# First loads in halves, the second batch's k turned on TensorE, and another step order, in an attention kernel with a gated feed-forward

## The chip, the cores and the metric

The kernel runs on one core of one Trainium2 chip. The time is device time in microseconds for one execution of the whole program. The median of three runs of the kernel before the change is 373.25 us (373.04 to 373.4).

## The reference

Eight batches of eight heads with 576 tokens of 64 numbers go through a linear attention with a learned feature map; the result feeds a gated feed-forward layer over all 4608 tokens.

```
def phi(x):
    proj = np.einsum('bhsd,df->bhsf', x, w_phi)               # 64 -> 128
    proj = proj - np.max(np.abs(proj), axis=-1, keepdims=True)
    return np.concatenate([np.exp(proj), np.exp(-proj)], axis=-1)
q_p, k_p = phi(q), phi(k)
kv  = np.einsum('bhsf,bhsd->bhfd', k_p, v)
z   = np.sum(k_p, axis=2)
num = np.einsum('bhsf,bhfd->bhsd', q_p, kv)
den = np.einsum('bhsf,bhf->bhs', q_p, z)[..., None] + 1e-06
x   = (num / den) laid out as [4608, 512]
out = (np.maximum(x @ w_gate, 0.0) * (x @ w_val)) @ w_out     # 512 -> 1536 -> 512
```

## The kernel before

The order of all work is written out by hand: `ORDER` is a string of some two thousand words, and a loop at the end of the kernel calls one small function for each, in that order. A word such as `ke.0.1.3.1:6@kp1` names the function (`do_ke`), its arguments (batch 0, head group 1, chunk 3, sign 1), after the colon the PSUM banks it uses, and after @ the buffer that it takes from a ring. Each engine runs its own instructions strictly in this order; waits between engines follow from the data and the buffers. The transfers stand in the same order on the queue of the engine that issues them: SyncE's queue takes `lf`, `wq`, `lw`, the `lv` of all batches but 0, the transposing transfers `xt` and the outputs `od`; GpSimd's takes `lk`, `lq`, `lm`, `ln`, `wl`, `wo` and batch 0's `lv`, and GpSimd issues them between its own computing.

A batch has 512 "main" tokens, in four chunks of 128, and 64 "rest" tokens. The heads are handled in three groups, `HEADS = ((0, 2), (2, 5), (5, 8))`; group 0 also carries the rest tokens. These are the steps for one batch `b`, group `j`, chunk `i`:

- Loads: `lk`, `lq`, `lv` bring k, q, v; `lm`, `ln`, `lw` bring their rest tokens (`lm` of batch 0 goes to a buffer of its own, `km0`, in another layout than `km`); `lf` brings k of batch 0, group 1 in full precision into a region that later holds `xTm`; `wq` brings `w_phi` twice, into rows 0 to 63 and 64 to 127 of `w64f`; `wl` and `wo` bring the feed-forward weights. Batch 1's v lies in a region that later holds `xTs`.
- Turning k: `kt` (L549) and `ku` (L554) transpose in blocks of 32x32 on VectorE, and `kr` (L565) projects with 24 matmuls of 32 rows and the weights `w32`. Batch 0 goes another way: `k0` (L587) is six 128x128 transposes on TensorE, `k1` (L590) copies them to SBUF on VectorE, and `k3` (L641) projects with six matmuls of 64 rows and the weights `w64`; `do_k2` (twelve such matmuls in one step) is defined and unused. The very first k (`lf`) is turned in full precision by `kf` (L618) and copied by `kg` on VectorE or `kh` on ScalarE. `wd` (L404) makes `w64` out of `w64f`; `sl`, `w1` and `wa` make `w32`.
- `ke` (L661, ScalarE) takes the exponentials of k's projection, `kx` (L669, VectorE) their maxima, `kk` the scale factors, `vs`, `vo`, `vq` (GpSimd) scale v (for batch 0 also `vd`, `vp`, `vz` on VectorE), `kv` (L767) multiplies, and `kc` copies the result to SBUF.
- q: `q0`, `q1`, `qb` (L813) for batch 0, `qt` and `qc` (L827) for the others, then `qe` (ScalarE), `qx` (VectorE) and the small `qy`, `qz`, `qu`, `qw`.
- The quotient: `nu` (L890, TensorE), `nt` (L911) and `nv` (L921) on VectorE, `nr` (L929, the reciprocal), `nx` (L933, GpSimd).
- x is transposed for the feed-forward: `xp` (L970, TensorE) and `xa` (L984, ScalarE) for batch 0, `xt` for the others.
- Feed-forward: `pv` and `pg` (L1093) for batch 0 by quarters of its tokens, `fv` and `fg` (L1064) for the rest, `va`, `ga`, `pa`, `pb` to empty the banks, `fo` (L1125) and the copies `oc`, `oe` to the output.
- `zz.n` (L428) is n matmuls on a tile of zeros that nobody reads: filler in places where TensorE would stand still. They add up to 76.

The first feed-forward matmul in the order is `pv.1.0`. From there on the order mixes the attention of batch b + 1 with the feed-forward of batch b.

## Time and profile before

| | |
|---|---|
| median of three runs | 373.25 us (373.04 to 373.4) |
| the profiled execution | 371.81 us |
| its span, first to last instruction | 370.0 us |
| granted TensorE clock, mean | 1.000 |
| VectorE, ScalarE, GpSimd busy | 289.0, 227.1, 156.5 us |

"PE" is TensorE, "PEld" its weight loads, "DVE" VectorE, "ACT" ScalarE, "POOL" GpSimd, "SP" SyncE; a "q" behind an engine's name means its instruction queue, such as the issue of a transfer. Matmuls overlap in the profile: the duration of one is longer than the distance from its start to the next one's start. VectorE's and ScalarE's instructions overlap by some 0.08 us in the same way. In a timeline a row merges neighbours of one kind (xN), and the brackets give the idle time before it and what ended that.

### The profile page before, as it was taken

The page shows a single profiled execution, that of the slowest core. Times are in us where ns is not written, and L with a number is a line of the kernel's source. Part 1 is how long each engine was busy: PE and PEld are TensorE (multiplying, and loading weights), DVE is VectorE, ACT ScalarE, POOL GpSimd, SP SyncE. Part 2 cuts the span into 40 slices and gives each one's busy share as a digit, 9 for nine tenths or more (in the row PEclk, how much of TensorE's full clock was granted, in tenths as well). Part 3 has the DMA queues.
Part 4 walks back from the last instruction along what each step waited for, and adds up shares of the span by engine and source line. Part 5 has one row for each costly group of instructions (what it writes and reads, how often), then busy time and mean ns, then how long its engine had stood idle before and what let it go on. Part 6 is the DMA issues. An engine that isn't in the chain of part 4 may idle for free.

```text
span 370.0 us, 9211 instructions
## 1 busy us (share of the span) xinstructions
PE 363.5 (98%) x3615; PEld 195.2 (53%) x3615; DVE 289.0 (78%) x674; ACT 227.1 (61%) x550; POOL 156.5 (42%) x161
## 2 busy tenths in 40 slices
...
GB/s 143 258 202 192 179 183 152 172 39 172 110 109 123 159 128 76 86 172 100 58 101 117 14 144 57 37 122 58 127 68 14 2 73 96 48 0 25 33 28 142
DMA packets 90380, 38.09 MB, mean 103 GB/s; under 512 B 64226, under 2 KB 85602, under 8 KB 90338
## 3 DMA queue, kind: packets, MB, share of 16 engines
...
q14 instruction: 14, 0.11, 0.1%
HBM read 37.81 MB, written 9.44 MB: 128 GB/s over the span
## 4 chain that ended last, share of the span: by engine, by line
PE 94%; DVE 2%; DMA 1%; ACT 1%; issue 0%; SPq 0%; ACTq 0%
PE bank L1064 47%; PE bank L1125 25%; PE bank L767 5%; PE bank L890 4%; PE bank L1093 4%; PE bank L565 3%; PE bank L827 2%; DMA w64f<-in_w_phi_dram 1%; PE bank L428 1%; ACT kp L661 1%; DVE h L850 1%; PE bank L1046 1%; PE bank L1156 1%; DVE vr L651 0%; PE bank L813 0%; PE bank L860 0%
## 5 line engine op out<-in xcount | busy, mean ns | idle before, releaser
L1125 PE MATMUL bank<-wo,h 128*128 128x512 bf16 x420 | 97.8, 379 | 0.0
L661 ACT ACTIVATE kp<-bank 128x384 bf16<-128x384 f32 x192 | 84.3, 518 | 15.3 <-PE bank L565 9.9
L1079 ACT CAST val<-bank 128x512 bf16<-128x512 f32 x81 | 47.2, 595 | 73.7 <-PE bank L1064 65.1
L1085 DVE SCALAR_TENSOR_TENSOR h<-bank,val 128x512 bf16<-128x512 f32 x100 | 66.8, 678 | 28.1 <-PE bank L1064 14.2
L1064 PE MATMUL bank<-xTs,wv 128*128 128x512 bf16 x352 | 87.1, 379 | 0.0
L1064 PE MATMUL bank<-xTs,wg 128*128 128x512 bf16 x352 | 86.3, 379 | 0.0
L933 POOL TENSOR_TENSOR xu<-u,r 128x512 bf16<-128x512 f32 x36 | 37.3, 1041 | 96.0 <-DVE r L929 54.3
L842 ACT ACTIVATE qp<-bank 128x512 bf16<-128x512 f32 x128 | 69.2, 620 | 10.7 <-PE bank L827 9.4
L718 POOL TENSOR_TENSOR vs<-vn,ek 128x780 bf16<-128x780 f32 (+2 forms) x40 | 53.7, 1363 | 23.8 <-ACT ek L678 13.3
L1125 PEld LDWEIGHTS <-h 128*128 128x128 bf16 x420 | 39.1, 98 | 45.9 <-issue 2.4
L1064 PEld LDWEIGHTS <-wg 128*128 128x128 bf16 x400 | 37.4, 98 | 41.4 <-issue 0.7
L1064 PEld LDWEIGHTS <-wv 128*128 128x128 bf16 x400 | 36.9, 98 | 40.4 <-issue 0.7
L669 DVE TENSOR_REDUCE mk<-bank 128x3 f32<-128x384 f32 x96 | 49.6, 539 | 2.5 <-ACT kp L661 1.3
L850 DVE TRANSPOSE_TENSOR_REDUCE maxq<-bank 128x16 f32<-128x512 f32 x56 | 37.4, 691 | 6.2 <-ACT qp L842 3.3
L921 DVE TENSOR_TENSOR u<-bank,t 128x195 f32<-128x195 f32 (+1 forms) x108 | 33.8, 329 | 2.8 <-POOL xu L933 0.6
L911 DVE TENSOR_TENSOR t<-bank,cq 128x195 f32<-128x195 f32 (+1 forms) x96 | 30.1, 323 | 6.8 <-PE bank L890 5.9
L890 PEld LDWEIGHTS <-qp 128*128 128x128 bf16 x512 | 23.1, 98 | 12.6 <-issue 2.0
L890 PE MATMUL bank<-kv,qp 128*128 128x65 bf16 x512 | 26.1, 193 | 0.3 <-ACT kv L778 0.2
L1134 ACT COPY ob<-bank 128x512 f32<-128x512 f32 x19 | 11.3, 596 | 22.2 <-PE bank L1125 22.1
L1137 DVE COPY ob<-bank 128x512 f32<-128x512 f32 x16 | 10.9, 683 | 16.1 <-PE bank L1125 13.8
...
L767 PEld LDWEIGHTS <-kp 128*128 128x128 bf16 x640 | 21.6, 97 | 2.8 <-ACT qp L842 0.2
...
## 6 DMA issues: line engine op xcount, KB each, us to landing
out_dram<-ob SPq DMA_DIRECT2D x31, 256.0 KB, 2.4
vn<-in_v_dram SPq DMA_DIRECT2D x24, 256.0 KB, 4.4
kn<-in_k_dram POOLq DMA_DIRECT2D x7, 512.0 KB, 9.2
qn<-in_q_dram POOLq DMA_DIRECT2D x7, 512.0 KB, 7.3
wv<-in_moe_w_val_dram POOLq DMA_DIRECT2D x3, 512.0 KB, 8.8
wg<-in_moe_w_gate_dram POOLq DMA_DIRECT2D x3, 512.0 KB, 8.7
wo<-in_moe_w_out_dram POOLq DMA_DIRECT2D x3, 512.0 KB, 7.6
...
```

Of the source, the lines that this page charges most:

```text
L661: nc.scalar.activation(kp_of(3 * b + j)[:, i, s].rearrange("p n f -> p (n f)"), bank[bk[0]][:, 0 : 3 * F], AF.Exp, scale=(1.0, -1.0)[s],)
L669: nc.vector.tensor_reduce(mk_of(3 * b + j)[:, :, i], bank[bk[0]][:, 0 : 3 * F].rearrange("p (n f) -> p n f", f=F), axis=AX.X, op=ALU.max, ...
L718: nc.gpsimd.tensor_tensor(vs_of(3 * b + j)[:, s, 0:n].rearrange("p n i e -> p (n i) e")[:, :, 0:e], src[:, lo:hi].rearrange("p h i e -> p ...
L767: nc.tensor.matmul(out_ps[:, h - lo, s, :], lhsT=lhsT, rhs=rhs, start=(at == 0), stop=(at == 2 * n * (C + 1) - 1),)
L842: nc.scalar.activation(qp_of(4 * b + i)[:, s, 4 * hq : 4 * hq + 4].rearrange("p h m -> p (h m)"), bank[bk[0]], AF.Exp, scale=(1.0, -1.0)[s],)
L850: nc.vector.tensor_reduce((maxq0[:, i] if b == 0 else maxq)[:, :, i, 4 * hq : 4 * hq + 4].rearrange("p t h -> p h t"), bank[bk[0]].rearran ...
L890: nc.tensor.matmul(bank[bk[0]][:, E * n : E * (n + 1)], lhsT=qp_of(4 * b + i)[:, s, h, :], rhs=kv_of(b)[:, h, s, 0:E],)
L933: eng.tensor_tensor(xu_of(n).rearrange("p (h d) -> p h d", d=D), u_of(n)[:, :, 0:D], r_of(n).to_broadcast([P, H, D]), op=ALU.mult,)
L1064: nc.tensor.matmul(bank[bk[0]], lhsT=w[:, dc, P * f : P * f + P], rhs=xT(g)[:, dc, :], start=(dc == 0), stop=(dc == NDC - 1),)
L1079: nc.scalar.copy(val_of(NFC * g + f), bank[bk[0]])
L1085: nc.vector.scalar_tensor_tensor(h2_of(g, f), bank[bk[0]], 0.0, val_of(NFC * g + f), op0=ALU.max, op1=ALU.mult)
L1125: nc.tensor.matmul(bank[bk[0]], lhsT=h2_of(g, f)[:, P * t : P * t + P], rhs=wo_sb[:, f, :], start=(f == 0), stop=(f == NFC - 1),)
```

## The change

Four things are different. `w_phi` comes in two transfers of 64 rows each, and the first k in two halves of two chunks each; both kinds alternate on SyncE's queue (`lf.1 wq.0 lf.0 wq.1`). Batch 1's k is turned as batch 0's is: three steps `k0.1.j`, `k1.1.j`, `k2.1.j` (twelve matmuls) stand in place of `kt.1.j`, `ku.1` and `kr.1.j`, and its rest tokens go to `km0`. Batch 1's v is loaded by head group with four tokens of a head to a partition (1 KB pieces) in three transfers, where it was loaded by chunks of 128 tokens (256 B pieces) in four. And `ORDER` is another one: up to about batch 2 the steps stand in another sequence, from batch 3 on it is nearly the same sequence with other banks and buffers. The filler adds up to 74 matmuls. The steps that make `w32` (`w1`, `wa`) move from the opening to just before `k2.1.1`.

```diff
--- before.py
+++ after.py
...
-ms.0 lf ms.2 lm.0.0 ms.4@vr0 ms.6 id lk.0.2 lk.0.0 wq ms.3@vr1 if ms.5 zz.12:7 kf.0:0 ms.9 kf.1:1 wd
-kh.0:0@kT0 sl k3.1.0:23 ke.0.1.0.0:2@kp0 w1:4 kg.1:1 kx.0.1.1:3@mk0 kx.0.1.0:2 wa:4 zz.2:7 k3.1.1:56
-ke.0.1.3.0:6 lm.0.1 kx.0.1.2:5 zz.3:7 k0.2:0 lq.0.1 ke.0.1.3.1:6 k1.2:0@kT1 ke.0.1.0.1:2 zz.3:7
-k0.0:1 ke.0.1.2.1:5 ke.0.1.1.1:3 k3.2.1:42 ke.0.1.2.0:5 kx.0.1.3:6 k1.0:1@kT2 zz.5:7 k3.0.1:06
-kk.0.1.0@ek0 k3.0.0:15 ke.0.1.1.0:3 ke.0.0.3.0:6@kp1 q0.1:3 lw.0.1 lq.0.0 kx.0.2.3:2@mk1 kx.0.2.2:4
-kk.0.1.1 ke.0.2.2.0:4@kp2 kx.0.0.0:1@mk2 kx.0.0.2:0 lv.0.1 ke.0.2.2.1:4 ke.0.0.1.1:5 kx.0.0.3:6
-q1.1:3@qT0 ke.0.0.1.0:5 ke.0.0.3.1:6 lv.0.0 zz.6:7 q0.0:4 kx.0.0.1:5 wl.0.1 zz.4:7 k3.2.0:36 lv.0.2
-ke.0.2.3.0:2 ke.0.0.2.1:0 ke.0.0.0.1:1 q1.0:4@qT1 ke.0.2.3.1:2 kx.0.2.1:6 zz.1:7 qb.1.1:5 zz.3:7
-qb.0.1:4 kx.0.2.0:3 ke.0.0.0.0:1 zz.2:7 qb.0.0:2 qx.0.0.1:4 ke.0.0.2.0:0 zz.1:7 qb.1.0:1 qx.0.1.1:5
-zz.7:7 qy.0.1:0 kp.0.0.0:2 ke.0.2.0.0:3 lk.1.3 kk.0.2.1@ek1 lw.0.0 kp.0.0.1:2 kk.0.2.0 ke.0.2.1.1:6
-vo.1@vs0 qx.0.1.0:1 qe.0.0.1.0:4@qp0 ke.0.2.0.1:3 qe.0.0.1.1:4 lq.1.2 qe.0.1.0.0:1@qp1 qe.0.1.0.1:1
-vs.0.1.0 qz.0.1:0@my0 zz.4:7 qb.0.3:0 qx.0.0.0:2 zz.2:7 qy.0.0:3 vd.0.0.0:2@vs1 qz.0.0:3@my1
-vs.0.1.1 qe.0.1.1.1:5 vp.0:2 qu.0.1@mz0 ke.0.2.1.0:6 qe.0.1.1.0:5 wl.0.0 vz.0:2 qb.0.2:4 zz.2:7
-qb.1.3:3 zz.2:7 qb.1.2:1 vd.0.0.1:2 qu.0.0@mz1 vz.1:2 qe.0.1.3.0:3@qp2 vo.2@vs2 qw.0.0@cq0
-qx.0.0.3:0 qx.0.0.2:4 qe.0.0.0.0:2 vs.0.2.1 zz.7:7 kv.0.0:6 qx.0.1.3:3 lw.1.1 vs.0.2.0 kc.0.0:6@kv0
-kt.1.1@kT3 qe.0.0.0.1:2 kv.0.2:5 kv.0.1:6 qe.0.0.2.1:4@qp3 lm.1.1 kc.0.2:5 wl.1.1 kc.0.1:6
-nu.0.0.0:2 nt.0.0.0:2@t0 zz.1:7 nu.0.0.2:5 qw.0.1 qx.0.1.2:1 qe.0.0.2.0:4 qe.0.1.3.1:3 nu.0.0.1:6
-nv.0.0.0:2@u0 zz.2:7 nu.0.1.2:4 lv.1.2 nu.0.1.0:2 qe.0.1.2.1:1 nt.0.0.1:6@t1 lm.1.0 nt.0.0.2:5@t2
-qy.0.2:3 nv.0.0.1:6 qe.0.0.3.0:0 nv.0.0.2:5 nt.0.1.0:2@t3 zz.2:7 nu.0.1.1:6 qy.0.3:5 nr.0.0@r0
-qe.0.1.2.0:1 qz.0.2:3@my2 nv.0.1.0:2@u1 qz.0.3:5@my0 qu.0.2@mz2 zz.5:7 kr.1.1:3125 qe.0.0.3.1:0
-nt.0.1.2:4@t0 nt.0.1.1:6@t1 qw.0.2 wl.1.0 nu.0.2.2:0 nx.0.0@xu0 nv.0.1.2:4 xp.0.0:7 nv.0.1.1:6
-nt.0.2.2:0@t2 ke.1.1.3.1:5@kp3 nr.0.1@r1 nu.0.2.1:4 xa.0.0:7 nt.0.2.1:4@t3 nu.0.2.0:6 ke.1.1.0.1:3
-nt.0.2.0:6@t0 qu.0.3@mz1 ke.1.1.0.0:3 pv.1.0:7 nv.0.2.1:4@u2 nv.0.2.2:0 nv.0.2.0:6 nu.0.3.1:4 qw.0.3
-ke.1.1.1.0:1 nx.0.1@xu1 kx.1.1.0:3@mk3 xp.0.1:0 pa.1.0:7@val0 kx.1.1.3:5 pv.0.0:6 nr.0.2@r2 xa.0.1:0
-nt.0.3.1:4@t1 nu.0.3.0:3 kx.1.1.1:1 nt.0.3.0:3@t3 ke.1.1.3.0:5 nu.0.3.2:7 kx.1.1.2:2 pa.0.0:6@val1
-nt.0.3.2:7@t2 pv.1.1:0 nx.0.2@xu2 lw.1.0 nv.0.3.0:3@u0 xp.0.2:5 ke.1.1.1.1:1 pv.0.1:6 nv.0.3.2:7
-pa.1.1:0@val2 pg.1.0:1 qt.1.1@qT2 ku.1@kT2 kk.1.1.0@ek2 ke.1.1.2.1:2 nv.0.3.1:4 pa.0.1:6@val3 lm.2.0
-kt.1.0 nr.0.3@r0 nx.0.3@xu3 kk.1.1.1 qc.1.1:3076 ke.1.1.2.0:2 wl.0.2 pg.1.1:4 xa.0.2:5 pv.0.2:2
-vo.1.1@vs3 qx.1.1.0:3 wl.1.2 pb.1.0:1 qe.1.1.1.0:0@qp4 qe.1.1.3.1:6@qp1 qe.1.1.0.0:3@qp0
-qe.1.1.1.1:0 qx.1.1.2:7 pa.0.2:2@val0 xp.0.3:5 pb.1.1:4 qx.1.1.1:0 qe.1.1.0.1:3 ln.0.1 qe.1.1.3.0:6
-pv.1.2:1 xc.0.3:5 pg.0.0:2 lm.2.1 kr.1.0:4305 lv.1.3 pa.1.2:1@val2 kt.1.2@kT1 qe.1.1.2.0:7@qp3
-ke.1.0.3.1:5@kp2 ln.0.0 pb.0.0:2 qe.1.1.2.1:7 ke.1.0.0.0:4 pv.0.3:1 kx.1.0.1:3@mk4 qx.1.1.3:6
-ke.1.0.2.0:0 lv.1.0 ke.1.0.2.1:0 pg.0.2:2 kx.1.0.0:4 qt.1.0@qT1 kx.1.0.2:0 ke.1.0.3.0:5 pg.0.1:7
-pb.0.1:7 pa.0.3:1@val1 pv.1.3:6 ke.1.0.1.0:3 pg.1.3:1 kx.1.0.3:5 ke.1.0.1.1:3 ke.1.0.0.1:4
-qc.1.0:0374 pb.0.2:2 pg.1.2:5 pa.1.3:6@val3 fv.0.9:6 pg.0.3:2 pb.1.3:1 kk.1.0.0@ek3 qx.1.0.0:0
-kk.1.0.1 pb.1.2:5 qx.1.0.1:3 qe.1.0.3.0:4 lk.2.3 lv.1.1 vs.1.1.1 qe.1.0.3.1:4 qe.1.0.2.1:7 vs.1.1.0
-qx.1.0.3:4 qe.1.0.0.0:0 qe.1.0.0.1:0 fv.0.10:1 va.0.9:6@val0 wo.0 vq.1.0 kr.1.2:5046 vq.1.1 pb.0.3:2
...
+ms.0 lf.1 wq.0 lf.0 ms.6 lm.0.0 ms.3@vr0 wq.1 ms.5 id lk.0.0 if ms.9 zz.9:7 kf.1:0 lm.0.1 ms.4@vr1
+lw.0.0 zz.1:7 kf.0:1 kg.1:0@kT0 wd k3.1.1:23 kh.0:1 ms.2 k3.1.0:45 sl lk.0.2 zz.8:7 k0.0:6
+ke.0.1.2.1:2@kp0 lq.0.0 ke.0.1.2.0:2 kx.0.1.3:3@mk0 kx.0.1.1:5 kx.0.1.0:4 k1.0:6@kT1 lq.0.1
+kx.0.1.2:2 zz.5:7 k3.0.1:01 ke.0.1.3.0:3 ke.0.1.1.1:5 ke.0.1.1.0:5 ke.0.1.0.1:4 k0.2:5 ke.0.1.0.0:4
+kx.0.0.2:0@mk1 k1.2:5@kT2 ke.0.1.3.1:3 ke.0.0.3.0:1@kp1 lv.0.0 k3.0.0:64 kx.0.0.0:6 kk.0.1.1@ek0
+kk.0.1.0 zz.4:7 k3.2.1:23 ke.0.0.2.1:0 ke.0.0.1.1:4 ke.0.0.0.1:6 lw.0.1 lv.0.1 q0.0:5 kx.0.0.3:1
+kx.0.2.3:3@mk2 q1.0:5@qT0 ke.0.0.2.0:0 ke.0.2.2.0:2@kp2 zz.6:7 q0.1:0 ke.0.0.3.1:1 ke.0.2.2.1:2
+qb.0.0:5 kx.0.0.1:4 lv.0.2 ke.0.0.0.0:6 qb.0.2:1 kp.0.0.0:5 wl.0.0 q1.1:0@qT1 kx.0.2.2:2 qx.0.0.2:1
+zz.4:7 k3.2.0:60 ke.0.0.1.0:4 ke.0.2.3.0:3 kx.0.2.1:0 ke.0.2.0.1:6 kp.0.0.1:5 ke.0.2.3.1:3 qb.1.0:4
+qe.0.0.2.0:1@qp0 qe.0.1.0.1:4@qp1 ke.0.2.1.1:0 kx.0.2.0:6 vp.0:5@vs0 vo.1@vs1 qb.1.3:2 ke.0.2.0.0:6
+qx.0.0.0:5 vd.0.0.0:5 qx.0.1.0:4 zz.26:7 qy.0.0:3 lk.1.3 vz.0:5 vz.1:5 kk.0.2.1@ek1 lq.1.2
+qe.0.0.2.1:1 kk.0.2.0 qz.0.0:3@my0 ke.0.2.1.0:0 wl.0.1 vs.0.1.0 wl.1.1 qe.0.1.0.0:4 vd.0.0.1:5
+vs.0.1.1 qb.1.2:6 qu.0.0@mz0 zz.1:7 kv.0.1:1 kv.0.0:0 qe.0.1.2.1:6 qe.0.1.2.0:6 vo.2@vs2 lm.1.1
+qe.0.0.0.1:5 kc.0.0:0@kv0 qb.0.1:4 qw.0.0@cq0 qe.0.0.0.0:5 vs.0.2.0 qx.0.1.2:6 qx.0.1.3:2 vs.0.2.1
+kc.0.1:1 lm.1.0 qb.0.3:3 qx.0.0.1:4 qy.0.2:6 qb.1.1:0 qe.0.0.1.0:4@qp2 qz.0.2:6@my1 zz.1:7 k0.1.1:5
+qe.0.1.1.0:0 qx.0.0.3:3 k1.1.1:5@kT3 kv.0.2:1 wl.1.0 nu.0.0.0:6 ln.0.0 nu.0.0.1:5 qe.0.0.1.1:4
+qx.0.1.1:0 nt.0.0.0:6@t0 lv.2.1 nt.0.0.1:5@t1 kc.0.2:1 zz.3:7 nu.0.0.2:4 qy.0.3:1 nv.0.0.0:6@u0
+nv.0.0.1:5 nt.0.0.2:4@t2 zz.1:7 qy.0.1:6 qe.0.1.1.1:0 nu.0.1.1:0 nu.0.1.0:5 qe.0.0.3.0:3@qp3
+qz.0.1:6@my2 zz.2:7 nu.0.1.2:6 nv.0.0.2:4 qe.0.1.3.0:2 qu.0.1@mz1 nr.0.0@r0 qw.0.1 qz.0.3:1@my0
+qu.0.2@mz2 qe.0.0.3.1:3 nx.0.0@xu0 nu.0.2.2:4 nt.0.1.0:5@t3 nt.0.1.1:0@t0 qe.0.1.3.1:2 nt.0.1.2:6@t1
+lm.2.0 nv.0.1.1:0@u1 w1:1 nv.0.1.0:5 zz.1:7 nu.0.2.0:3 zz.2:7 xp.0.0:7 nv.0.1.2:6 qw.0.2
+nt.0.2.0:3@t2 wa:1 lw.1.0 k2.1.1:2015 nu.0.2.1:6 nr.0.1@r1 qu.0.3@mz0 xa.0.0:7 nt.0.2.2:4@t0
+ke.1.1.1.1:0@kp3 nv.0.2.0:3@u2 nx.0.1@xu1 qw.0.3 ke.1.1.2.0:1 nt.0.2.1:6@t3 nv.0.2.2:4 pv.1.0:7
+nu.0.3.0:3 xp.0.1:4 ke.1.1.3.0:5 nv.0.2.1:6 kx.1.1.1:0@mk3 ke.1.1.2.1:1 lm.2.1 nr.0.2@r2 kx.1.1.2:1
+nx.0.2@xu2 pv.0.0:6 xa.0.1:4 kx.1.1.3:5 pa.1.0:7@val0 ke.1.1.1.0:0 lw.1.1 pv.1.1:4 nt.0.3.0:3@t1
+nu.0.3.1:1 nu.0.3.2:7 qt.1.1@qT2 ke.1.1.3.1:5 ln.0.1 nv.0.3.0:3@u0 xp.0.2:0 pa.0.0:6@val1
+pa.1.1:4@val2 nt.0.3.1:1@t2 xa.0.2:0 ke.1.1.0.0:2 k0.1.2:5 nt.0.3.2:7@t0 pg.1.0:6 nv.0.3.1:1
+nv.0.3.2:7 pb.1.0:6 wl.0.2 nr.0.3@r0 qc.1.1:3401 ke.1.1.0.1:2 k1.1.2:5@kT1 qe.1.1.3.1:1@qp4
+qx.1.1.2:0 pv.0.2:7 kx.1.1.0:2 nx.0.3@xu3 pg.1.1:6 qe.1.1.0.1:3@qp1 qe.1.1.3.0:1 pa.0.2:7@val3
+kk.1.1.1@ek2 xp.0.3:5 qx.1.1.0:3 pv.1.2:2 qe.1.1.2.1:0@qp2 xc.0.3:5 pb.1.1:6 k0.1.0:7
+qe.1.1.1.0:4@qp0 qe.1.1.1.1:4 qx.1.1.3:1 qx.1.1.1:4 pg.1.3:5 k1.1.0:7@kT2 qe.1.1.0.0:3 kk.1.1.0
+qt.1.0@qT0 lv.1.1 pv.1.3:6 pa.1.2:2@val0 qe.1.1.2.0:0 k2.1.0:1342 pa.1.3:6@val2 ke.1.0.1.0:3@kp0
+ke.1.0.2.0:4 kx.1.0.0:1@mk4 ke.1.0.2.1:4 kx.1.0.3:2 pb.1.3:5 ke.1.0.1.1:3 ke.1.0.0.0:1 pg.0.0:7
+pg.0.2:0 pb.0.0:7 kx.1.0.1:3 ke.1.0.3.1:2 lv.1.2 pv.0.1:6 kx.1.0.2:4 lk.2.3 lv.1.0 vs.1.1.1@vs3
+pv.0.3:5 mt.0 ke.1.0.3.0:2 ke.1.0.0.1:1 ms.1 pb.0.2:0 qc.1.0:7231 pg.0.1:4 pa.0.1:6@val2
+kk.1.0.0@ek3 wl.1.2 qx.1.0.1:2 pg.0.3:6 fv.0.10:0 pa.0.3:5@val1 qe.1.0.0.1:7 kk.1.0.1 fv.0.9:5
+vs.1.1.0 qe.1.0.3.0:1 qx.1.0.3:1 vo.1.1 qe.1.0.2.1:3 vs.1.0.0@vs1 qe.1.0.1.0:2 qe.1.0.0.0:7 vq.1.0
+pb.0.3:6 qx.1.0.2:3 ku.2@kT3 qe.1.0.3.1:1 vo.1.0 vq.1.1 qe.1.0.1.1:2 wo.1 pb.0.1:4 va.0.9:5@val3
+lm.3.1 fv.0.11:6 va.0.10:0@val1 k2.1.2:1245 va.0.11:6@val2 wo.0 ke.1.2.2.0:4@kp2 qx.1.0.0:7
...
@@ -388,11 +389,11 @@
                 stop=(a == 1),
             )
 
-    def do_wq(bk):
-        nc.sync.dma_start(out=w64f, in_=w_phi[None].to_broadcast([2, D, F]))
-
-    def do_wr(bk):
-        nc.scalar.dma_start(out=w64f, in_=w_phi[None].to_broadcast([2, D, F]))
+    def do_wq(bk, half):
+        nc.sync.dma_start(out=w64f[D * half : D * (half + 1)], in_=w_phi)
+
+    def do_wr(bk, half):
+        nc.scalar.dma_start(out=w64f[D * half : D * (half + 1)], in_=w_phi)
 
     def do_wc(bk):
         nc.vector.tensor_copy(w32.rearrange("p a f -> p (a f)"), bank[bk[0]][:, 0 : 2 * F])
@@ -443,11 +444,12 @@
         flat = xT_mix.rearrange("p a b -> p (a b)").bitcast(FP32)[:, 0 : 3 * C * D]
         return flat.rearrange("p (h x) -> p h x", h=3)
 
-    def do_lf(bk):
+    def do_lf(bk, cp):
         lo, hi = HEADS[1]
+        c2 = slice(2 * cp, 2 * cp + 2)
         nc.sync.dma_start(
-            out=k_first().rearrange("p h (c d) -> p h c d", d=D),
-            in_=k[0, lo:hi, 0:SF, :].rearrange("h (p c) d -> p h c d", c=C),
+            out=k_first().rearrange("p h (c d) -> p h c d", d=D)[:, :, c2],
+            in_=k[0, lo:hi, 0:SF, :].rearrange("h (p c) d -> p h c d", c=C)[:, :, c2],
         )
 
     def cast_first(copy, half):
@@ -472,7 +474,7 @@
         )
 
     def do_lm(bk, b, hh):
-        if b == 0:
+        if b < 2:
             nc.gpsimd.dma_start(
                 out=km0[SM * hh : SM * (hh + 1)],
                 in_=k[b, hh::2, SF:S, :].rearrange("i t d -> t i d"),
@@ -498,6 +500,12 @@
             lo, hi = HEADS[i] if i < 3 else (HEADS[1][0], HEADS[2][1])
             nc.gpsimd.dma_start(
                 out=v_flat()[:, lo:hi],
+                in_=v[b, lo:hi, 0:SF, :].rearrange("h (p c) d -> p h c d", c=C),
+            )
+        elif b == 1:
+            lo, hi = HEADS[i]
+            nc.sync.dma_start(
+                out=v_in(b)[:, lo:hi],
                 in_=v[b, lo:hi, 0:SF, :].rearrange("h (p c) d -> p h c d", c=C),
             )
         else:
@@ -570,12 +578,12 @@
                         stop=(n == 2 and a == 1),
                     )
 
-    def do_k0(bk, j):
-
+    def do_k0(bk, *bj):
+        b, j = bj if len(bj) == 2 else (0, *bj)
         pt = bank[bk[0]].bitcast(BF16)
         lo, hi = HEADS[j]
         blocks = [
-            kn_of(0)[:, h, 2 * cp : 2 * cp + 2, :].rearrange("p c d -> p (c d)")
+            kn_of(b)[:, h, 2 * cp : 2 * cp + 2, :].rearrange("p c d -> p (c d)")
             for h in range(lo, hi)
             for cp in range(2)
         ]
@@ -586,18 +594,21 @@
         for n, blk in enumerate(blocks):
             nc.tensor.matmul(pt[:, P * n : P * n + P], lhsT=blk, rhs=ident, is_transpose=True)
 
-    def do_k1(bk, j):
+    def do_k1(bk, *bj):
+        b, j = bj if len(bj) == 2 else (0, *bj)
         nc.vector.tensor_copy(
-            kT_of(j).rearrange("p n m a -> p (n m a)"), bank[bk[0]].bitcast(BF16)[:, 0 : 6 * P]
-        )
-
-    def do_kw(bk, j):
+            kT_of(3 * b + j).rearrange("p n m a -> p (n m a)"), bank[bk[0]].bitcast(BF16)[:, 0 : 6 * P]
+        )
+
+    def do_kw(bk, *bj):
+        b, j = bj if len(bj) == 2 else (0, *bj)
         nc.scalar.copy(
-            kT_of(j).rearrange("p n m a -> p (n m a)"), bank[bk[0]].bitcast(BF16)[:, 0 : 6 * P]
-        )
-
-    def do_k2(bk, j):
-        T = kT_of(j).rearrange("p n m a -> p (n m a)").rearrange("p (k m) -> p k m", m=P)
+            kT_of(3 * b + j).rearrange("p n m a -> p (n m a)"), bank[bk[0]].bitcast(BF16)[:, 0 : 6 * P]
+        )
+
+    def do_k2(bk, *bj):
+        b, j = bj if len(bj) == 2 else (0, *bj)
+        T = kT_of(3 * b + j).rearrange("p n m a -> p (n m a)").rearrange("p (k m) -> p k m", m=P)
         heads = [1, 2, 0] if j == 0 else [0, 1, 2]
         first = set()
         for k_, n in enumerate(heads):
```

403 lines of the change are left out of this document (201 added, 202 removed).

## The prediction

> **What bounds the kernel now.** I read the page first, then the kernel in windows, then the waits of TensorE, then the timeline of the first 30 us.
>
> ```profile
> span 370.0 us, 9211 instructions
> PE 363.5 (98%) x3615; PEld 195.2 (53%) x3615; DVE 289.0 (78%) x674; ACT 227.1 (61%) x550; POOL 156.5 (42%) x161
> ...
> L428 PE MATMUL bank<-zero 128*128 128x256 bf16 x76 | 13.1, 297 | 1.1 <-DVE zero L414 1.1
> ...
> 6.00:10.00 4.00, 3.69 (x57) 2.63 (x56) 4.00 (x10) 3.33 (x10) 4.00 (x6) 1.00 1.45 183
> ...
> 22.00:26.00 4.00, 3.74 (x71) 3.01 (x67) 3.97 (x14) 3.97 (x10) 1.55 (x3) 1.00 1.26 206
> 26.00:30.00 4.00, 3.76 (x88) 3.38 (x86) 4.00 (x18) 3.75 (x11) 1.76 (x2) 1.00 1.26 195
> 30.00:34.00 4.00, 4.00 (x76) 3.45 (x74) 3.98 (x12) 3.80 (x11) 1.53 (x2) 1.00 1.18 223
> ...
> 300.00:340.00 40.00, 40.00 (x206) 18.46 (x205) 18.52 (x40) 7.12 (x13) 4.13 (x4) 1.00 0.16 46
> ...
> PE bank L641 <- DVE w L404: 1.1, 1, 1.1
> ...
> PE bank L618 <- DMA xTm<-in_k_dram: 0.5, 1, 0.5
> PE bank L1093 <- ACT xTs L984: 0.2, 1, 0.2
> ```
>
> In the windows the columns are length, then busy time of PE, PEld, DVE, ACT and POOL, then granted clock. The kernel has two parts. From about 28 us to the end TensorE is full (4.00 of 4.00, 40.00 of 40.00) at clock 1.00, and its last wait over 0.15 us is the one on `xTs` L984. There the end moves only with TensorE's own work. Before that VectorE and ScalarE are full, and TensorE's busy time is partly filler: the 76 matmuls on `zero` (L428) compute nothing. So the opening is paced by VectorE and ScalarE. Whatever brings the first real FFN matmul (`pv.1.0`, L1093) forward comes off the end, and whatever adds to TensorE's work behind it goes on top.
>
> ```profile
> 0.74 0.45 SPq L448 DMA_DIRECT2D xTm<-in_k_dram  x1
> ...
> 1.24 0.73 SPq L392 DMA_DIRECT2D w64f<-in_w_phi_dram  x1
> ...
> 4.31 0.89 PE L618 MATMUL bank<-identf,xTm 128*128 128x128 f32 x6 [0.52 <-DMA xTm<-in_k_dram]
> ...
> 5.92 0.33 DVE L404 CAST w<-w64f 128x128 bf16<-128x128 f32 x1 [2.37 <-DMA w64f<-in_w_phi_dram]
> ...
> 6.30 0.34 PE L641 MATMUL bank<-w,kT 64*128 64x128 bf16 x6 [1.10 <-DVE w L404]
> 6.31 0.53 DVE L627 CAST kT<-bank 128x384 bf16<-128x384 f32 x1
> ...
> 6.77 1.47 DVE L669 TENSOR_REDUCE mk<-bank 128x3 f32<-128x384 f32 x3
> ...
> 25.42 0.17 DVE L929 RECIPROCAL r<-u 128x8 f32<-128x8 f32 x1
> ...
> 25.68 1.03 POOL L933 TENSOR_TENSOR xu<-u,r 128x512 bf16<-128x512 f32 x1 [2.45 <-DVE r L929]
> ...
> 26.15 0.55 PE L565 MATMUL bank<-w,kT 32*128 32x128 bf16 x24
> 26.63 0.36 PE L890 MATMUL bank<-kv,qp 128*128 128x65 bf16 x6
> 26.82 0.39 PE L970 MATMUL bank<-ident,xu 128*128 128x128 bf16 x4
> ...
> 27.25 0.58 ACT L984 COPY xTs<-bank 128x512 bf16<-128x512 bf16 x1
> ...
> 27.88 1.05 PE L1093 MATMUL bank<-xTs,wv 128*128 128x128 bf16 x16 [0.24 <-ACT xTs L984]
> ```
>
> The chain reads: `w_phi` is issued at 1.24 and lets VectorE go at 5.92, 4.66 us later, although the k piece in front of it is ready at 4.31. VectorE idles 2.37 us for it. From 6.77 (first `kx`) VectorE runs without a break worth naming to the reciprocal at 25.42 (`nr.0.0`), which is 18.65 us of work. Then come `nx.0.0` on GpSimd, `xp.0.0` on TensorE at 26.82, `xa.0.0` on ScalarE, and `pv.1.0` at 27.88.
>
> **The change: the opening loads.** SyncE's queue now carries four transfers where it had two: `lf.1`, `wq.0`, `lf.0`, `wq.1`. At the pitch of the two rows above (0.74 to 1.24, 0.50 us) the fourth is issued at 2.24, against 1.24 for the whole `w_phi` before. The two `lw` behind it start some 1 us later than before; only `vz`, much later, needs their data. The price of a half `w_phi` is in no row. Slow end: it takes as long as the k piece from issue to use (0.74 to 4.31, 3.57 us), so 5.8 us, and nearly nothing is won. Fast end: it lands directly behind the k bytes, which were there at 4.31 and are now followed by 64 KB, a sixth more: about 4.5 us. In the new order VectorE takes `kg.1` before `wd`. `kg.1` waits for one half of k, its three transposes (0.6 us, as from 4.31 to ScalarE's turn copy before) and its own 0.53 us. With half the bytes ahead of it I put that half near 3.9, a little before 4.31, so `wd` starts no earlier than 5.0. I take 5.0, nearer the fast end, because 64 KB taking longer than 384 KB looks like the shape of that one transfer, not the queue. So the opening wins 0.9 us, bounds 0.1 to 1.3 us, and the first `kx` stands at 5.9.
>
> **VectorE from there to `nr.0.0`.** The two orders hold the same VectorE steps in front of `nr.0.0` but for two: `kt.1.1` becomes `k1.1.1`, and an `nt` of 0.27 changes places with a `qz` of 0.23.
>
> ```profile
> L549 DVE STREAM_TRANSPOSE kT<-kn 128x384 f32<-128x384 f32 x14 | 12.0, 860 | 0.0
> ...
> L549 DVE STREAM_TRANSPOSE kT<-kn 128x256 f32<-128x256 f32 x7 | 4.3, 613 | 0.0
> L554 DVE STREAM_TRANSPOSE kT<-km 128x128 f32<-128x128 f32 x7 | 2.0, 280 | 0.0
> L590 DVE COPY kT<-bank 128x768 bf16<-128x768 bf16 x2 | 1.1, 542 | 0.0
> ```
>
> That is 0.86 − 0.54 = 0.32 us less, and with the other swap 0.35: 18.65 − 0.35 = 18.3, so `nr.0.0` starts at 5.9 + 18.3 = 24.2 instead of 25.42. `nx.0.0` and `xp.0.0` follow as before (1.40 us from `nr.0.0` to `xp.0.0`): 25.6. ScalarE starts 0.9 earlier too and has one `ke` less ahead of `xa.0.0`, so it is there before 27.25 − 0.9 = 26.35, by about 25.9. `xa.0.0` then runs 0.43 after `xp.0.0` as before (26.82 to 27.25), at 26.0, and `pv.1.0` at 26.0 + 0.63 = 26.65 (27.25 to 27.88). That is 1.23 us earlier. The filler changes from 76 matmuls to 74, one block being of 26; all of it stands ahead of `pv.1.0` where TensorE waits, so I cost it at nothing. The block of 26 is about 2.9 us (0.11 each, twice the 0.056 of a `k0` transpose below, which is half as wide); if it ran past its release, `qy.0.0` would be late by the excess.
>
> **TensorE's own work.** Three `kr` (24 matmuls) go; three `k0` (6 transposes) and three `k2` (12 matmuls) come.
>
> ```profile
> 7.61 0.50 PE L587 MATMUL bank<-ident,kn 128*128 128x128 bf16 x6
> ...
> 7.95 0.49 PE L428 MATMUL bank<-zero 128*128 128x256 bf16 x3
> ...
> 9.69 0.51 PE L641 MATMUL bank<-w,kT 64*128 64x128 bf16 x12
> ...
> 10.34 0.61 PE L795 MATMUL bank<-ident,qn 128*128 128x128 bf16 x8
> ```
>
> A `kr` holds TensorE from 26.15 to 26.63: 0.48 us. A `k0` from 7.61 to 7.95: 0.34. A burst's span holds the drain of its last matmul, 0.50 − 0.34 = 0.16; the twelve L641 span 0.51, so a `k2` is 0.35, taken as 0.34. Ahead of `pv.1.0` the change trades one `kr` for one `k0` and one `k2` where TensorE has filler to give; behind it, where TensorE is full, 2 × (0.34 + 0.34 − 0.48) = 0.40 us is added to the end. Bounds: 0.2, if a `k2` costs per matmul what a `kr` does (12 of 24, 0.24), to 1.0, if each of the four added bursts pays the 0.16 of drain.
>
> The Trainium skill speaks against this step: "TensorE: Matmul & The Clock Gate", Part 4 (PE-mode transpose), gives about 275 ns for one 128x128 transpose inside a kernel, and says that such work does not count as busy for the clock. By that figure a `k0` would cost 1.65 us, an estimate from that page, and the two behind `pv.1.0` would make the sum 2.6 us dearer. The trace has 0.34 us and clock 1.00, so I go by the trace.
>
> The other VectorE savings (`kt.1.0`, `kt.1.2`, `ku.1` for two `k1`: 0.61 + 0.86 + 0.28 − 1.08 = 0.67 us) fall behind `pv.1.0`, beside a full TensorE: nothing. They are slack, worth up to 0.67 us if TensorE should come to wait for VectorE there.
>
> **The v of batch 1.** It leaves SyncE as three transfers with 1 KB pieces instead of four with 256 B pieces, and it stands behind `lv.2.1` and the two `lw.1`. `lv.2.1` waits there for the last `vs.0.2` to have read its buffer, so all of them go out from about 21 us on.
>
> ```profile
> kn<-in_k_dram POOLq DMA_DIRECT2D x1, 512.0 KB, 10.6
> ...
> vn<-in_v_dram POOLq DMA_DIRECT2D x2, 384.0 KB, 7.6
> ...
> xTs<-in_v_dram SPq DMA_DIRECT2D x4, 256.0 KB, 11.4
> ```
>
> 256 KB in small pieces needed 11.4 us to land, 384 KB in 1 KB pieces from the other queue 7.6. At 7.6 us each, behind one another, they are there in the low thirties. Batch 1's `vs` on GpSimd is what would be late, and TensorE's first `kv.1` behind it; no wait of TensorE hangs on it before, so I cost it at nothing.
>
> **Sum.** −1.23 + 0.40 = −0.83 us: span 370.0 to 369.2, the profiled execution from 371.81 to 370.98. The median of the runs is 1.44 us above that execution, so 373.25 becomes 372.4. A measurement of this kernel tells about 0.2%, 0.75 us, from no change.
>
> **Rivals.**
> (A) The data sets the pace, not `w_phi`. The first q turned on TensorE started at 10.34 when its data came, and batch 1's k was issued at 9.14 and needed 10.6 us, until 19.7; both lie behind the same bytes in GpSimd's queue as before. VectorE has ten steps of `kx` and `k1` ahead of its first q copy, at the 0.465 us that three of them show from start to start ((1.47 − 0.54) / 2), so it wants q at 5.9 + 4.65 = 10.55; turned, it is there at 10.34 + 0.45 = 10.8. `k0.1.1` now stands on TensorE ahead of `kv.0.2` and every `nu`. For it: both are within 0.3 us of deciding. Against: neither is late by much. If they eat 0.9 of the 1.23 us, −0.33 + 0.40: 373.3.
>
> (B) Slower: GpSimd becomes the bound.
>
> ```profile
> 9.14 0.96 POOL L437 DMA_DIRECT2D kn<-in_k_dram  x1
> ...
> 12.49 0.88 POOL L469 DMA_DIRECT2D qn<-in_q_dram  x1 [1.38 <-PE bank L795]
> ...
> 17.37 2.90 POOL L718 TENSOR_TENSOR vs<-vn,ek 128x768 bf16<-128x768 f32 x2
> 20.22 0.75 POOL L481 DMA_DIRECT2D km<-in_k_dram  x1
> ```
>
> Between `lq.1.2` and the last `vs.0.2` the new order puts one more load of weights (0.81) and `lm.1.1` (0.75): 20.27 becomes 21.8, or 21.1 if `lq.1.2` comes 0.7 earlier with the earlier q. `kv.0.2`, then `nu.0.0.0` and all `nt` stand behind it on TensorE and VectorE. From that end to `nr.0.0` there were 5.15 us (to 25.42); 24.2 − 21.1 leaves 3.1, about what `kv.0.2`, a `nu` and three pairs of `nt` and `nv` need. So it decides from about 21.1 on, microsecond for microsecond: at 23.0, 372.4 + 1.9 = 374.3.
>
> (C) The transposes do not overlap: each holds TensorE for its own 0.22 us (0.50 less five starts of 0.056), so a `k0` is 1.3 instead of 0.34, and the two behind `pv.1.0` add 1.9: 374.3. The page of the Trainium skill named above would have it so; the L587 row speaks against it.
>
> (D) More: `w_phi` at the fast end (0.4 us more), the 0.24 us wait ahead of `pv.1.0` gone and VectorE's 0.67 us put to use by TensorE: 371.5.
>
> **Chances.** Forecast 0.48 (its own range 371.9 to 372.9, 0.30 of it over 0.2% faster), A 0.17, B 0.18, C 0.02, D 0.15. Faster by over 0.2% (under 372.5): 0.30 + 0.15 and a little of A, 0.48. Within: 0.31. Slower (over 374.0): 0.21. The range 371.2 to 374.3 leaves out the far half of B and the end of D.
>
> **What would show it.** Right: `wd` near 5.0, first `kx` near 5.9, `nr.0.0` near 24.2, `pv.1.0` near 26.7, TensorE full behind it, `k0` and `k2` 0.34 us each. Wrong: `wd` past 5.6 (loads), a VectorE gap before `q1` or `nt.0.0.0` (A, B), waits of TensorE on `vs`, `kv` or `kT` between 28 and 60 us, where VectorE and ScalarE are nearly full too: that cover is thin, and each such wait goes straight to the end.

## The result, and the profile after

| | before | changed |
|---|---|---|
| median of the runs | 373.21 us (373.04 to 373.4, 4 runs) | 375.62 us (375.45 to 376.08, 4 runs) |
| ratio to before | | 1.0075, 95% interval 1.0051 to 1.0099 |
| the profiled execution, its span | 371.81, 370.0 us | 375.67, 373.8 us |

The change makes the kernel slower by 2.4 us by the medians (a ratio of 1.0065, inside the interval). The two profiled executions lie 3.86 us apart, because that of before is one of its fastest (why is the first experiment's matter); their spans lie 3.77 us apart, and the traces show where these are. First TensorE's opening, from its timeline (start, duration; L429 is the filler `zz`, L629 `kf`, L652 `k3`, L595 `k0`):

```profile
1.05 2.10 PE L429 MATMUL bank<-zero 128*128 128x256 bf16 x9 [1.05 <-DVE zero L415]
3.37 0.88 PE L629 MATMUL bank<-identf,xTm 128*128 128x128 f32 x3 [0.21 <-DMA xTm<-in_k_dram]
...
5.00 0.90 PE L629 MATMUL bank<-identf,xTm 128*128 128x128 f32 x3 [0.55 <-DMA xTm<-in_k_dram]
5.83 1.14 PE L652 MATMUL bank<-w,kT 64*128 64x128 bf16 x12
6.90 1.89 PE L429 MATMUL bank<-zero 128*128 128x256 bf16 x8
8.59 0.63 PE L595 MATMUL bank<-ident,kn 128*128 128x128 bf16 x4
...
9.23 1.24 PE L429 MATMUL bank<-zero 128*128 128x256 bf16 x5
...
11.38 0.61 PE L429 MATMUL bank<-zero 128*128 128x256 bf16 x4
```

The prediction's row has three filler matmuls at 7.95 in 0.49 us, 0.11 from one to the next (0.49 less a drain of 0.16). Here the eight at 6.90 take 1.89, 0.21 each, and those at 11.38 are back at 0.61 for four, 0.11 each. TensorE runs at half its rate until the five at 9.23 are nearly done, about 10.3 us; before it was at the full rate from 4.4 on (`kf`'s six matmuls at 4.31 took 0.89 us there; the three at 5.00 take 0.90 here). VectorE waits for it:

```profile
5.22 0.28 DVE L405 CAST w<-w64f 128x128 bf16<-128x128 f32 x1 [0.39 <-DMA w64f<-in_w_phi_dram]
...
6.40 1.64 DVE L680 TENSOR_REDUCE mk<-bank 128x3 f32<-128x384 f32 x3 [0.75 <-PE bank L652]
9.47 0.56 DVE L599 COPY kT<-bank 128x768 bf16<-128x768 bf16 x1 [1.43 <-PE bank L595]
...
26.60 0.20 DVE L940 RECIPROCAL r<-u 128x8 f32<-128x8 f32 x1
...
29.05 0.72 PE L1104 MATMUL bank<-xTs,wv 128*128 128x128 bf16 x10
```

`wd` is at 5.22 (before 5.92) and the first `kx` at 6.40 (6.77), but `k1.0` then waits 1.43 us for `k0.0`, which stands behind the filler. `nr.0.0` is at 26.60 and `pv.1.0` at 29.05, 1.17 us later than before.

Behind `pv.1.0` there is one long wait of TensorE, at 74 us. The view of its waits (total, times, longest), then its timeline, then SyncE's queue:

```profile
PE bank L1075 <- DMA xTs<-xu: 1.2, 1, 1.2
```

```profile
74.13 1.24 PE L1075 MATMUL bank<-xTs,wv 128*128 128x512 bf16 x5 [1.17 <-DMA xTs<-xu]
```

```profile
61.95 1.44 SPq L512 DMA_DIRECT2D vn<-in_v_dram  x2
63.48 6.69 SPq L976 DMA_TRANSPOSE xTs<-xu  x2
...
70.89 1.21 SPq L976 DMA_TRANSPOSE xTs<-xu  x1
```

`lv.2.2` and `lv.2.0` go out one behind the other, and the issue of the next two transposing transfers (`xt.1.1`, `xt.1.2`) then takes 6.69 us, so that the last one starts at 70.89. Before, three of them took less:

```profile
62.51 5.06 SPq L965 DMA_TRANSPOSE xTs<-xu  x3
```

The third and fourth part are TensorE's work and the end. The timeline of before:

```profile
37.84 0.51 PE L565 MATMUL bank<-w,kT 32*128 32x128 bf16 x24
38.29 0.51 PE L1093 MATMUL bank<-xTs,wv 128*128 128x128 bf16 x6
...
367.30 0.38 ACTq L1172 DMA_DIRECT2D out_dram<-ob  x1
```

And of the changed kernel:

```profile
37.46 0.39 PE L595 MATMUL bank<-ident,kn 128*128 128x128 bf16 x4
37.69 0.28 PE L595 MATMUL bank<-ident,km 128*128 128x128 bf16 x2
37.80 1.06 PE L1104 MATMUL bank<-xTs,wg 128*128 128x128 bf16 x16
...
39.71 0.51 PE L619 MATMUL bank<-w,kT 64*128 64x128 bf16 x12
40.15 1.07 PE L1104 MATMUL bank<-xTs,wg 128*128 128x128 bf16 x16
...
370.64 0.37 ACTq L1183 DMA_DIRECT2D out_dram<-ob  x1
```

A `k0` holds TensorE 0.34 us (37.46 to 37.80), a `k2` 0.44 (39.71 to 40.15), a `kr` held it 0.45 (37.84 to 38.29): 2 × (0.34 + 0.44 − 0.45) = 0.66. And the tail: from the issue of the last transfer (`d1`) to the end of the span it is 370.0 − 367.30 = 2.7 us before and 373.8 − 370.64 = 3.15 after, though that transfer lands 1.8 us behind its issue in both.

So the spans' 3.77 us are: opening 1.17; waits behind `pv.1.0` 1.17 and one of 0.15 at 170 us; tail 0.43; and 0.85 that are left for TensorE's work, of which 0.66 are the steps above. The other 0.2 is a remainder that no row shows by itself.

### The profile page after: what moved, and what is told of

Same layout as the page of the kernel before. It is cut to its first block, busy times and chain, and to the rows that moved or that the text cites. A ratio compares the mean times of both kernels' runs of the same rounds, so it can differ in the third digit from the quotient of the medians.

```text
span 373.8 us, 9159 instructions
## 1 busy us (share of the span) xinstructions
PE 366.4 (98%) x3595; PEld 197.3 (53%) x3595; DVE 289.4 (77%) x673; ACT 227.4 (61%) x550; POOL 156.5 (42%) x161
## 4 chain that ended last, share of the span: by engine, by line
PE 89%; DVE 4%; ACT 3%; DMA 2%; issue 1%; SPq 0%; POOL 0%; DVEq 0%; ACTq 0%; POOLq 0%
PE bank L1075 45%; PE bank L1136 23%; PE bank L778 4%; PE bank L901 4%; PE bank L1104 4%; PE bank L838 2%; PE bank L573 2%; ACT kp L672 1%; DVE mk L680 1%; PE bank L429 1%; DMA xTm<-in_k_dram 1%; DMA xTs<-xu 1%; PE bank L1167 1%; ACT qp L853 1%; PE bank L1057 1%
## 5 line engine op out<-in xcount | busy, mean ns | idle before, releaser
L778 PE MATMUL bank<-vs,kp 128*128 128x65 bf16 x512 | 22.5, 194 | 0.2 <-DVE vs L710 0.2
```

The source lines that it names most:

```text
L778: nc.tensor.matmul(out_ps[:, h - lo, s, :], lhsT=lhsT, rhs=rhs, start=(at == 0), stop=(at == 2 * n * (C + 1) - 1),)
```

## The experiments

The kernels were timed in four sets, each on one chip and beside the kernel before, whose medians were 373.03, 373.15, 372.6 and 372.92 us (28 to 35 executions each, 371.8 to 374.4 in the first). The first set holds `e1`, `e2`, `e3` and `e5`, the second `e4`, `e6`, `e7` and `e8`, the third `e9` to `e12`, the fourth `e13` to `e15`; across sets, tenths of a us say little. A profile shows one execution, and where it is not a typical one of its kernel, this is said.

### TensorE's rate in the opening

`e1_fill` closes the gaps of the filler in the changed kernel.

```diff
-... ms.9 zz.9:7 kf.1:0 ... lw.0.0 zz.1:7 kf.0:1 kg.1:0@kT0 wd k3.1.1:23 kh.0:1
+... ms.9 zz.11:7 kf.1:0 ... lw.0.0 zz.5:7 kf.0:1 zz.2:7 kg.1:0@kT0 wd k3.1.1:23 zz.2:7 kh.0:1
```

> The changed kernel with nine more filler matmuls in the opening, so that TensorE has no gap from 1.05 us to the first k3 (11 instead of 9 ahead of kf.1, 5 instead of 1 between kf.1 and kf.0, 2 ahead of k3.1.1, 2 ahead of k3.1.0). Theory H1 (the gaps that the new order of loads leaves in the filler keep TensorE at its slow rate until 10.3 us; the eight filler matmuls ahead of k0.0 then take 1.89 us instead of 0.88, the five behind it 1.24 instead of 0.55): the filler's pitch falls from 0.213 to 0.109 us by about 7 us, k0.0 ends about 1 us earlier, nr.0.0 about 1.5 us earlier, median about 374.0 us (373.5 to 374.6) against 375.6 for the changed kernel. Rival R1 (the opening is late because the data of q and k or VectorE's own steps are late, whatever TensorE's rate): 375.6, or slower by what the extra filler adds, 375.6 to 376.2.

Measured: 375.16 us (374.42 to 375.48). Its timeline of TensorE:

```profile
6.59 1.05 PE L419 MATMUL bank<-zero 128*128 128x256 bf16 x8
...
27.66 1.05 PE L1094 MATMUL bank<-xTs,wv 128*128 128x128 bf16 x16
...
73.26 2.10 PE L1065 MATMUL bank<-xTs,wv 128*128 128x512 bf16 x9 [1.69 <-DMA xTs<-xu]
```

The eight filler matmuls take 1.05 instead of 1.89, and `pv.1.0` starts at 27.66, 1.39 earlier than in the changed kernel. But TensorE now waits 1.69 us at 73 us instead of 1.17: 0.5 us are given back to the transposes there. In the profile the theory holds (the execution is 0.85 us faster than the changed kernel's); by the median the gain is 0.46 us where 1.6 were expected, so the forecast of 373.5 to 374.6 was missed.

`e5_before_gap` does the opposite in the kernel before.

```diff
-... ms.5 zz.12:7 kf.0:0 ...
+... ms.5 zz.5:7 kf.0:0 ...
```

> The kernel before with 5 instead of 12 filler matmuls at its start, so that TensorE stands idle from about 2.1 to 4.3 us, and nothing else. H1: TensorE goes to its full rate 3 us or more later than 4.4 us, the filler ahead of k0 and q0 takes twice its time, and the kernel is 0.5 to 1.8 us slower: 373.8 to 375.0. Rival R1: fewer filler matmuls cost nothing: 373.2, within 0.3.

Measured: 373.88 us (373.25 to 374.79), ratio 1.001 to 1.0045.

```profile
1.06 1.25 PE L419 MATMUL bank<-zero 128*128 128x256 bf16 x5 [1.06 <-DVE zero L405]
4.25 1.51 PE L609 MATMUL bank<-identf,xTm 128*128 128x128 f32 x6 [1.95 <-DMA xTm<-in_k_dram]
...
7.91 0.82 PE L419 MATMUL bank<-zero 128*128 128x256 bf16 x3
9.16 0.85 PE L419 MATMUL bank<-zero 128*128 128x256 bf16 x3
```

`kf`'s six matmuls take 1.51 instead of 0.89, three filler matmuls 0.82 instead of 0.49, and `pv.1.0` is at 29.44 instead of 27.88. The span of this execution is 1.6 us longer than that of the fast profile of before; by the medians, seven matmuls that compute nothing are worth 0.85 us (373.88 against 373.03). Both lie in the forecast of H1.

`e4_before_fill` closes the gaps in the kernel before.

```diff
-... ms.5 zz.12:7 kf.0:0 ms.9 kf.1:1 wd ...
+... ms.5 zz.14:7 kf.0:0 ms.9 kf.1:1 zz.7:7 wd ...
```

> The kernel before with more filler in the opening and nothing else: 14 instead of 12 filler matmuls at the start and 7 new ones behind kf.1, where TensorE stood idle from 5.2 to 6.3 us. The 31 executions of the kernel before lie in groups, at 371.8, at 373.0 to 373.5 and at 374.1 to 374.4. H1 (the groups are executions in which TensorE reaches its full rate early or late, and a gap in the filler makes it late): the later groups vanish or shrink, median 371.8 to 372.5. Rival R1: the groups have another origin, median 373.0 as before, or 373.3 if the filler gets in the way of k3.

Measured: 371.93 us (371.79 to 373.32), ratio to before 0.9974, interval 0.9957 to 0.999. Of 12 executions one lies above 372.9, where 20 of the 35 of before in that set do. So most of the spread of the kernel before is in its opening, in the idle 0.5 and 1.1 us around `kf`. This is the fastest kernel of the study, faster than both.

What makes them fall well or badly is in the traces. They hold records of TensorE's granted clock, from the moment of the first full rate on, which the page does not list. The full rate first begins at (us):

```
gaps of 0.3 us at most up to the first k3:
  e7 4.13  e4 4.51  e8 4.68  e1 4.76  e12 4.83  e3 5.81  e13 6.28  e11 6.31  e10 6.95  e14 6.96  e9 7.15
larger gaps:
  before 4.43  e2 4.68  e6 9.57  e5 10.20  changed 10.30  (e15 4.39, see below)
```

Every stretch at one rate that lies inside a trace is 3.41 us long or a whole multiple of it (27.31, 365.23 and 368.64 are 8, 107 and 108 times 3.41). So the rate changes on a raster of 3.41 us, and where the raster lies in the span differs from one execution to the next. Counting TensorE's idle time between two marks gives the rule that all 17 profiles follow: the full rate begins at the end of the first stretch with at most 0.56 us of idle time (before 0.56, `e2_lv` 0.43, `e7_fill_lv2` 0.34); a stretch with 0.68 us or more (the changed kernel 0.68, `e9_tail` 0.73, `e6_lv2` 0.85) is followed by another one at half rate. Nothing between 0.56 and 0.68 was seen.

`e2_lv`, which has the opening of the changed kernel word for word, shows what that means. Its marks fell at 1.26 and 4.68, it had the full rate from 4.68 on, and its `pv.1.0` is at 27.62, as early as with the gaps closed. In the changed kernel they fell at 3.47, 6.88 and 10.30. Idle times of 0.55 and 0.13 us lie between the first two, and the full rate came with the third. So the gaps do not make the rate late each time; they make it a matter of luck.

The Trainium skill, "TensorE: Matmul & The Clock Gate", Part 1, says that TensorE is at half rate until it was busy through one window of some 3.4 us, and that the windows run freely, so that the moment varies. The traces agree, though a stretch need not be wholly without gaps: without larger gaps TensorE is at the full rate by 7.2 us in all eleven profiles (two windows behind the first matmul at 1.06 would end by 7.9, an estimate).

The kernel before shows the same in its times: of its 123 executions in the four sets, 11 have a mean granted clock of 0.995, as one stretch of 3.41 us at half rate in 371 us would give, and all 11 took 373.14 us or more. An execution whose first full rate is late has no such mark, so for the others that took as long the late rate is likely and not shown.

### The loads ahead of the transposes

`e2_lv` moves `lv.2.0`, `e6_lv2` moves `lv.2.2` too (the diff is that of `e6_lv2`).

```diff
-... my.0:6 mz.0:6@my1 fo.0.2.1:7 lv.2.2 nv.1.3.2:1 ... ke.2.1.2.0:4 lv.2.0 kx.2.0.0:0 ... xt.1.3 ke.2.2.3.0:1
+... my.0:6 mz.0:6@my1 fo.0.2.1:7 nv.1.3.2:1 ... ke.2.1.2.0:4 kx.2.0.0:0 ... xt.1.3 lv.2.2 lv.2.0 ke.2.2.3.0:1
```

> The changed kernel with one word moved: lv.2.0, a load of v in 256 B pieces, stands behind xt.1.3 on SyncE's queue instead of ahead of xt.1.1. Theory H2 (two such loads issued 0.6 us apart fill the queue, so that the issue of the transpose behind them takes 5.26 us instead of 1.78, the next two are late with it, and TensorE waits 1.2 us at 73 us): xt.1.1 issues in under 2.5 us, the wait of TensorE at 73 us is gone, 1.2 us less: 374.4 us (374.2 to 374.7). Rival R2 (TensorE would wait there for another thing, or the time lost at 73 us is given back by slack later): 375.3 to 375.7.

Measured: 375.21 us (373.99 to 376.42), 0.4 us less than the changed kernel where 1.2 were expected; this is nearer to the rival's 375.3. The profile is that of its fastest execution. In it `xt.1.1` took 3.2 us to issue instead of 5.26, and TensorE's wait at 72 us was 0.63: about half of the theory. (The view names ScalarE's `qp` as what ended this wait; but in `e7_fill_lv2` the same matmul starts at 71.85 while that `qp` runs until 72.54, so it does not need it. That leaves the transposes.)

> The changed kernel with both loads in 256 B pieces (lv.2.2 and lv.2.0) behind xt.1.3 instead of ahead of xt.1.1. With lv.2.0 alone moved, xt.1.1 still took 3.2 us to issue and TensorE still waited 0.63 us instead of 1.17. H2: the second load has the rest; xt.1.1 issues in under 2 us, no wait of TensorE over 0.1 us at 72 us, 0.6 us less than with one load moved: 374.6 us by the median of that run (374.3 to 374.9). Rival R2 (the issue of xt.1.1 is long for another reason, for instance because it needs the transpose before it to be done): xt.1.1 still takes over 3 us, 375.2.

Measured: 374.39 us (373.27 to 375.44), within the 374.3 to 374.9 of H2. SyncE's queue:

```profile
60.39 4.68 SPq L966 DMA_TRANSPOSE xTs<-xu  x3
```

Three transposes in 4.68 us, `xt.1.1` among them in 1.87, and TensorE waits over 0.1 us for nothing between `pv.1.0` and 168 us. Both loads were in the way: the issue of `xt.1.1` takes 5.26, 3.2 and 1.87 us with two, one and none of them ahead. What on the queue makes it long is not shown.

`e3_both` is `e2_lv`, and `e7_fill_lv2` is `e6_lv2`, with the filler of `e1_fill`; `e8_fill_lv2_zz5` has `zz.5:7` for `zz.8:7` ahead of `k0.0` besides.

> Both edits together. If both theories hold and their gains add up: 375.6 - 1.6 - 1.2 = 372.8 us (372.2 to 373.3), about the kernel before. If they overlap (an earlier opening runs into the same transposes earlier): nearer 374.

Measured: 374.08 us (373.41 to 374.83), nearer the overlapping case; a wait of 0.38 us was left at 72 us, and `xt.1.1` took 4.15 us to issue, with the one load ahead.

> The changed kernel with the filler of the first experiment and both loads behind xt.1.3. H1 and H2 together: 374.1 (with one load) less the 0.38 us that TensorE still waited there: 373.7 us (373.3 to 374.0). What is then left over the kernel before is TensorE's added work behind pv.1.0, 0.7 us. If a rival of H2 holds: 374.1.

Measured: 373.46 us (373.33 to 374.64), as expected: opening and transposes together give back 2.2 us. Against `e4_before_fill`, the kernel before with its gaps closed, in the same set (371.93), 1.5 us are left. The spans of the two profiles differ by 1.40: tail 0.43, the wait at 168 us 0.15, TensorE's work the rest, and nothing from the opening, for `pv.1.0` is at 28.01 here and at 28.00 there.

> As the run before, with 5 instead of 8 filler matmuls ahead of k0.0. If the filler stands in the way of k0.0 (VectorE waited 0.28 us for it): k0.0 0.3 us earlier, 0.2 to 0.3 us less, 373.4. If k0.0 then waits for its data instead (the transfer of the first k): k0.0 at the same time, no change, 373.7.

Measured: 373.72 us (373.09 to 374.27). `k0.0` came 0.17 us earlier in the profile and `pv.1.0` 0.57, and the fastest execution is 0.24 faster; the median is 0.26 slower. The profile is that of its fastest execution, so neither case is shown.

### The tail

SyncE's last instructions wait once for every semaphore of the transfers. The trace's records of these waits, which the page does not list, end at (us):

```
before:  ... 368.40  368.78  369.14 (d1)
changed: ... 372.48 (d1)  372.54  372.61  372.67  372.73  372.79  372.85  372.91
```

The transfers of SyncE's and ScalarE's queues take eight semaphores in turn. The change has one such transfer more (two for the halves of k, two for `w_phi`, one fewer for v), so `d1` comes to the first of the list instead of the last, and seven waits of 0.06 us follow it. `e9_tail` is `e7_fill_lv2` with one output through GpSimd's queue; `e10_before_tail` is `e4_before_fill` with that output in two transfers.

```diff
-            nc.sync.dma_start(out=dst, in_=ob_of(4 * g + t))
+            q = nc.gpsimd if (g, t) in ((6, 1),) else nc.sync
+            q.dma_start(out=dst, in_=ob_of(4 * g + t))
```

> The changed kernel with the filler and with both loads behind xt.1.3 (373.5 us in its own runs), and one edit more: one output tile (od.6.1) leaves through GpSimd's queue instead of SyncE's, so that one transfer fewer takes its turn among the eight semaphores of SyncE's and ScalarE's queues. Theory H3: at the end SyncE waits for each semaphore in the order of their numbers, 62 ns each; in the changed kernel the count of transfers is one larger, the last transfer has the first number, and 0.43 us of waits for semaphores that are long done come behind it. With one fewer, the last transfer is last in the list again: the time from the issue of the last transfer to the end of the span falls from 3.15 to about 2.7 us, median about 373.05 (372.8 to 373.3). Rival: the longer tail comes from the last transfer itself or from the profiler: no change, 373.5.

> The kernel before with the filler (371.9 us in its own runs), and the same output tile as two transfers of half the rows, one transfer more. H3: the last transfer gets the first number, the tail grows by 0.43 us, median about 372.35 (372.2 to 372.5). Rival: 371.9.

The ends of the two timelines, `e9_tail` first, each with its span:

```profile
core 0 of [0], span 371.7 us
...
368.99 0.37 ACTq L1174 DMA_DIRECT2D out_dram<-ob  x1
```

```profile
core 0 of [0], span 371.3 us
...
368.10 0.37 ACTq L1169 DMA_DIRECT2D out_dram<-ob  x1
```

2.7 and 3.2 us (3.15 before rounding): the tail of the span follows the count of transfers, in both kernels. The times of the runs show it less well: `e9_tail` has a median of 373.7 (fastest 373.07, against 373.33 without the edit), `e10_before_tail` 373.02 (fastest 372.43, against 371.79). Both medians lie above the forecast by 0.65. One reason is the opening: in both profiles TensorE has the full rate only at 7 us. Another shows in the records of the single executions, which give the time and the span. In `e9_tail` the time is 2.4 us longer than the span (median), in `e7_fill_lv2` 2.0 and in the kernel before 1.8. So the median span got 0.2 us shorter, and what lies outside it 0.4 longer; why is open. That a shorter tail shortens the time as well is therefore not shown; that a longer one lengthens it, `e10_before_tail` supports.

### The opening's loads

`e12_open` puts only the new loads of `w_phi` and the first k into the kernel before, with gapless filler and, by outputs through GpSimd's queue, `d1` last in the list. `e14_wphi` has only `w_phi` in two (`lf`, `wq.0 wq.1`), `e15_halves` only the halves of k (`lf.0`, `wq lf.1`).

```diff
-ms.0 lf ms.2 ... lk.0.0 wq ms.3@vr1 if ms.5 zz.12:7 kf.0:0 ms.9 kf.1:1 wd
+ms.0 lf.0 ms.2 ... lk.0.0 wq.0 lf.1 wq.1 ms.3@vr1 if ms.5 zz.11:7 kf.0:0 zz.5:7 ms.9 kf.1:1 zz.2:7 wd
```

> The opening of the change alone: the kernel before with w_phi in two transfers and the first k in two halves, the filler kept without a gap (11, 5 and 2 matmuls), and two output tiles through GpSimd's queue so that the last transfer stays last in the list; batch 1 and the order behind the opening are those of before. If the earlier w_phi is worth what the prediction said (wd 0.7 us earlier, first kx 0.6 to 0.9 earlier, and VectorE's chain moves with it): pv.1.0 0.5 to 0.9 us earlier than with the filler alone, 371.1 to 371.5 us. Rival (q and the rest of k, which land as before, set the pace a few steps later): pv.1.0 within 0.2 us, 371.7 to 372.0.

Measured: 372.89 us (372.37 to 374.56). That is slower than both cases; the fastest execution is 0.6 us behind the fastest of `e4_before_fill` (371.79, in another set). The profile is that of the slowest of the twelve executions:

```profile
6.12 1.51 DVE L661 TENSOR_REDUCE mk<-bank 128x3 f32<-128x384 f32 x3
...
8.15 0.51 PE L579 MATMUL bank<-ident,kn 128*128 128x128 bf16 x6 [0.96 <-DMA kn<-in_k_dram]
...
13.28 0.62 PE L787 MATMUL bank<-ident,qn 128*128 128x128 bf16 x8 [1.01 <-DMA qn<-in_q_dram]
```

The first `kx` starts at 6.12, 0.65 earlier than before, as forecast. Then TensorE waits 0.96 us for the next k and 1.01 for q, and `pv.1.0` is at 29.44; in the other executions these waits are likely shorter. The view of the transfers has SyncE's and ScalarE's queue in the first 20 us (packets, MB, share), here and in the kernel before:

```profile
q1 hardware_dynamic: 1504, 0.59, 11.9%
```

```profile
q1 hardware_dynamic: 1074, 0.59, 10.8%
```

That is 430 packets more for the same bytes.

> The kernel before with w_phi in two transfers of 64 rows and nothing else of the change (the first k stays one load of 1 KB pieces), filler without a gap, last transfer last in the list. Theory H5 (it is the halves of the first k, in 512 B pieces, that make k and q late): wd at 5.0 to 5.4, first kx near 6.2, TensorE waits under 0.3 us for k and q, pv.1.0 0.4 to 0.7 us earlier than the 28.0 us of the filler alone, fastest runs 371.1 to 371.5, median 371.4 to 371.9. Rival (any earlier w_phi pushes k and q back, or they set the pace anyway): pv.1.0 at 27.8 or later, fastest runs 371.8 or more.

Measured: 372.51 us (371.86 to 373.99). No wait for k or q in the profile, as expected, but `wd` is at 5.72, not at 5.0 to 5.4: `w_phi` behind the whole first k is only 0.2 us earlier than in one transfer. The full rate came at 6.96 in this execution, so the first `kx` is at 7.18 and `pv.1.0` at 28.37. The fastest execution is at 371.86, as the rival had it: nothing is gained.

> The kernel before with the first k in two halves (512 B pieces) and w_phi as one transfer, filler without a gap, last transfer last in the list. H5: TensorE waits 0.5 us or more for k and about 1 us for q as with both cuts, pv.1.0 at 28.8 or later, fastest runs 372.4 or more. Rival: no wait of TensorE for k over 0.2 us, 371.8 to 372.1 in the fastest runs.

Measured: 375.18 us (372.82 to 376.85).

```profile
7.26 0.55 PE L610 MATMUL bank<-identf,xTm 128*128 128x128 f32 x3 [2.24 <-DMA xTm<-in_k_dram]
```

The loss is there, but at another place than expected: the second half of the first k, behind the undivided `w_phi`, is itself 2.24 us late. This gap also takes the full rate away again, as the windows of this run show (length, busy time of the five engines, granted clock, DMA):

```profile
4.40:7.80 3.40, 1.16 (x11) 0.81 (x9) 0.42 (x2) 0.48 (x1) 3.40 (x6) 1.00 1.11 155
7.80:11.20 3.40, 3.40 (x28) 1.88 (x26) 2.17 (x4) 1.50 (x4) 1.40 (x2) 0.50 1.43 201
11.20:14.00 2.80, 2.80 (x46) 2.15 (x44) 2.39 (x6) 2.59 (x9) 0.91 (x1) 1.00 1.15 303
```

TensorE is busy for 1.16 of 3.40 us in the first of these windows and has half its clock in the next. So the run does not isolate the effect of the pieces on k and q. Shown is, in the one execution of the profile, that the two cuts together bring the first `kx` forward and make the next k and q late; that the 512 B pieces do it is likely (1504 packets and 1474 with the halves, 1104 without), but only argued.

### Batch 1's k back on VectorE

`e11_kt` and `e13_kt2` take `kt`, `ku`, `kr` for `k0`, `k1`, `k2` in `e9_tail`, with v in four 256 B loads.

```diff
-... k0.1.0:7 ... k1.1.0:7@kT2 ... k2.1.0:1342 ... lv.1.0 ...
+... ku.1@kT2 kt.1.0 ... kr.1.0:1342 ... lv.1.0 lv.1.3 ...
```

`e13_kt2` also moves `lm.2.0` and `lm.2.1` behind `kt.1.0`.

> As e9_tail (filler, both loads behind xt.1.3, last transfer last in the list), and batch 1's k turned on VectorE again with its v in 256 B pieces (kt, ku and kr for k0, k1 and k2; two output tiles through GpSimd's queue keep the last transfer last). Theory H4 (TensorE's added work behind pv.1.0 is 0.65 us and goes straight to the end): 0.5 to 0.8 us less than e9_tail, about 372.4. Rival R4 (that stretch is as much VectorE's as TensorE's, or v in small pieces comes late): no gain or slower than e9_tail, 373.0 to 374.

Measured: 380.26 us (379.06 to 381.57). `lm.2.0`, whose buffer batch 1 now uses again, waited 4.1 us on GpSimd's queue, and `nx.0.1` behind it. It says nothing on H4.

> As e11_kt (batch 1's k turned on VectorE again, its v in 256 B pieces, filler, both loads behind xt.1.3, last transfer last in the list), with the two loads of batch 2's km behind the last reader of the buffer that they fill. H4: TensorE's stretch from pv.1.0 to kr.3.0 is 0.5 to 0.7 us shorter than the 55.4 to 55.6 us of the changed kernel, near the 54.6 of the kernel before; median 372.3 to 373.0, against 373.0 to 373.7 of e9_tail. Rival R4: TensorE waits for VectorE or for v there, the stretch is as long or longer, 373.5 or more.

Measured: 376.04 us (375.15 to 378.11). The stretch from `pv.1.0` to `kr.3.0` is 58.6 us: the rival.

```profile
50.42 0.19 PE L762 MATMUL bank<-vr,kp 128*128 128x65 bf16 x1 [0.86 <-POOL vr L741]
...
53.75 0.28 PE L762 MATMUL bank<-vs,kp 128*128 128x65 bf16 x4 [1.50 <-POOL vs L713]
...
43.14 1.47 POOL L713 TENSOR_TENSOR vs<-xTs,ek 128x768 bf16<-128x768 f32 x1 [1.89 <-DMA xTs<-in_v_dram]
```

GpSimd starts batch 1's `vs` at 43.14, 4 us later than the changed kernel does (39.13), and TensorE waits 2.4 us for it. Of the 4 us GpSimd waits 1.89 for v in small pieces; the rest comes from the two moved loads, which GpSimd can issue only at 38.89, when VectorE has turned batch 1's k. So the larger pieces of v are worth something in the new order, but this run mixes them with the moved loads. What the turn on TensorE costs by itself is read from the rows above (0.66 us) and was not shown by undoing it.

## Why the prediction was wrong

- **"All of it stands ahead of `pv.1.0` where TensorE waits, so I cost it at nothing."** This is the step that failed. The filler's count was right to ignore (74 for 76), its gaps were not. They leave TensorE at half rate until 10.3 us, the filler itself then stands in front of `k0.0`, and the opening loses 1.17 us instead of gaining 1.23. With the gaps closed (`e1_fill`, `e7_fill_lv2`) `pv.1.0` is at 27.7 and 28.0, and in `e2_lv`, where the full rate came early by luck, at 27.6.
- **−1.23 us from the earlier `w_phi`.** Even then only −0.2 to +0.1 is left. In `e1_fill` the missing 1.0 us is in three places. The first `kx` comes 0.64 us earlier instead of 0.87 (`wd` at 5.25, `kx` at 6.13). VectorE waits 0.63 us in all between there and `nr.0.0` (0.29 of it for `k0.0`), where it waited 0.27 before. And its work in between, waits taken out, is 18.46 us and was 18.39: the 0.35 us that I took off did not come, for the twelve `kx` take 0.3 to 0.4 us more than before. Rival A has about the right size (0.9 of the 1.23 us, at a chance of 0.17) but its mechanism only in part: TensorE waits 0.39 us for q's data in `e7_fill_lv2`, and not at all in `e1_fill`.
- **+0.40 us for `k0` and `k2`.** The mechanism was right, the size off: 0.66. The `k2` was mis-sized: I took the drain of a transpose, 0.16, off its span of 0.51, and it holds TensorE for 0.44; a `kr` holds it for 0.45 behind `pv.1.0`, not 0.48.
- **"TensorE full behind it."** Two terms were not in the sum: the loads ahead of the transposes (1.17 us in the profile; the prediction looked at SyncE's queue only for v of batch 1), and the last waits (0.43 of the span).
- **The base.** I added a constant 1.44 us from the profiled execution to the median. It is no constant: it is mostly what the gaps of before cost in its typical execution, and closing them takes the median to 371.93. So the fast draw of the profile hid that the kernel before had the same fault in its opening.
- **Held:** v of batch 1 at nothing, and `k0` at 0.34. **Rival B** fell: the last `vs.0.2` ended late, at 23.26, but VectorE had no wait over 0.1 us from 10.8 us to `nr.0.0`, so it decided nothing. **C** fell with `k0`'s 0.34, **D** with the opening. The Trainium skill's 275 ns for a transpose ("TensorE: Matmul & The Clock Gate", Part 4) is not what six transposes in 0.34 us show.
